# A long convolution by FFT beside local attention: the forward transforms in two passes, in place

## The chip, the core and the metric

The kernel runs on one core of a Trainium2 chip. The metric is the device time of one execution in microseconds (us); the table below gives the median of three executions. The profile is one further execution, whose span leaves out about 2 us that the device time has.

Five engines with their own instruction queues work in parallel and wait for each other through semaphores: TensorE (PE; its weight loads are shown apart as PEld), VectorE (DVE), ScalarE (ACT), GpSimd (POOL) and SyncE (SP, which here only issues transfers). TensorE writes its results to PSUM; ScalarE and VectorE copy them ("evict" them) to SBUF.

## The reference

Two branches share the input x and are mixed by a gate per position. S = 2048 positions, D = 640 channels, bfloat16.

```python
x = A_q
g = _sigmoid((x * gate_w).sum(-1, keepdims=True))
# branch a: short convolution of k (4 taps) times v, then a convolution with ssm_k as long as the sequence
kv = k_shift * v
kv_f = rfft(pad(kv, 2 * S));  kf_f = rfft(pad(ssm_k, 2 * S))        # along positions, per channel
y = irfft(kv_f * kf_f)[:S]
a = q * (y + kv * ssm_D)
# branch b: 32 heads of 20, each position attends to 8 positions at distance 0, 2, ..., 14
q, k, v = split(x @ wqkv);  b = softmax(q . k[idx] * scale) . v[idx] @ wo
out = g * a + (1 - g) * b
```

## The kernel before

The transform of 4096 points is done as two stages of small matmuls. Channels are held as 5 groups of 16 in the free dimension, 4 quarters and 2 halves, so that one tile of 4096 elements per partition is one group. Stage 1 ("s1") multiplies by `F1b`, stage 2 ("s2") by a matrix `G[:, j]` of its own for each of 32 frequencies j, with a real and an imaginary row (`rr`). The same code transforms h (the long filter) and u (the product k_shift * v).

```python
def s1_unit(key, src, g, oc, Am, free):          # 8 matmuls of 128 columns, one eviction of 1024
    ...
    copy(e.eng, Am[:, :, :, 4 * oc:4 * oc + 4]..., ps[:]...)

def s2_unit(dst, jb, Am, deps, free):            # one group, 8 frequencies: 32 matmuls of 64 columns
    for jj in range(8):
        j = 8 * jb + jj
        for rr in range(2):
            for c in range(2):
                rows = slice(64 * c, 64 * c + 64)
                o = ps[:, c, :].rearrange("p (q j l) -> p q j l", q=4, j=8)[:, :, jj, :]
                nc.tensor.matmul(o, lhsT=G[rows, j, rr, :], rhs=Am[rows, 2 * j + rr, :, :],
                                 start=(rr == 0), stop=(rr == 1), tile_position=(64 * c, 0), ...)
    copy(e.eng, dst[:, :, :, 8 * jb:8 * jb + 8, :]..., ps[:]...)   # one eviction of 1024

def transform(key, s2dst, s2free):               # s1 of group g+1 between s2 of group g
    for oc in range(4):
        yield from s1(0, oc)
    for g in range(NG):
        for jb in range(4):
            if g + 1 < NG:
                yield from s1(g + 1, jb)
            pdone, edone = yield from s2_unit(dst, jb, Am, evs, s2free(g, jb))
```

Stage 1 writes into one of two buffers `Am`, stage 2 from there into `Hs[g]` for h or, for u, into one buffer `Up` for all groups, which must have been multiplied before the next group may be written. The complex product needs h also with its partition halves swapped (`Hw`, by SyncE's transfers, line 844). VectorE multiplies per group and per quarter of the frequencies (lines 866 and 869):

```python
        for g in range(NG):
            for jb in range(4):
                nc.vector.tensor_tensor(v(Hs), v(Up), v(Hs), ALU.mult)
                nc.vector.tensor_tensor(v(Hw), v(Up), v(Hw), ALU.mult)
```

The first inverse stage ("i1", line 883) multiplies both products by `M`, 16 matmuls and one eviction for a quarter of a group; the second ("i2", line 960) uses `T`. The output projection of the attention ("op", line 999) runs per block of 128 positions, 16 blocks. Then y is multiplied by the gated x in `qg` and the attention is added, per two blocks, and stored:

```python
    def store(t):
        if t in (1, 5):
            return
        t0 = t - 3 if t < 8 else t - 1
        for gg in range(4):
            eng = nc.gpsimd if t < 4 and gg % 2 else nc.scalar if t == 15 and gg % 2 else nc.sync
            eng.dma_start(...)
```

The order on each engine is made while the program is built. Each part of the kernel is a generator that asks for an engine ("P", or "AD" for whichever of ScalarE and VectorE a small table of costs says is done first). `Plan` takes, of all that could go next, the one that can start first, with a handicap of 120 ns per unit of priority:

```python
                p = pri if r.pri is None else r.pri
                key = (st + 120.0 * p, p, k)
    ...
    plan.add(conv(), 6)
    plan.add(qkproj(), 3)
    plan.add(h_stream(), 5)
    plan.add(u_stream(), 5)
    plan.add(mults(), 1)
    plan.add(inverse1(), 4)
    ...
```

So the costs in `Plan` decide only the order; the chip then runs each queue in that order, waiting where data is not there. PSUM is used as four slots of two banks.

Of the kernel before, what the change touches and what calls it, by code (L numbers as in the profile page):

```python
# [48 lines left out]
def fft_consts():  # L49
# [3 lines left out]
    F1b = np.zeros((4, 32, 2, 64))  # L53
    for q in range(4):
        F1b[q, :, q % 2, :] = F1
# [89 lines left out]

MODE = dict(score_gen=1, h_stream=2, u_stream=2, inverse2=4)


class Plan:
# [33 lines left out]
    def fetch(self, st, cost, ins, keep=False):  # L183

        pages, t = list(self.page), st
        for c in range(len(pages), (self.count + ins) // 256 + 1):
            at = t + cost * (256 * c - self.count) / ins
            late = max(0.0, pages[-1] + 3500.0 - at)
            pages.append(at + late)
            t += late  # L190
        if keep:
            self.page, self.count = pages, self.count + ins
        return t + cost
# [10 lines left out]
    def run(self):  # L204
        while self.streams:
# [19 lines left out]
            self.at[e] = end  # L225
            if r.move:
                at = max(self.pipe, st + 1300.0)
                self.pipe = at + r.move
                g.done = Ev(self.pipe + 700.0, "X")
                self.lane[e].append(g.done.t)  # L230
# [13 lines left out]
def kernel(  # L244
# [280 lines left out]
    def vproj():  # L525
        for half in range(2):
            c0 = 320 * half
            for b0 in range(0, NB, 2):
                nb = min(2, NB - b0)
                g = yield Req("P", 5 * nb * 136.0, xdeps(min(3, (b0 + nb - 1) // 4)) + [ev(f"Wv{half}")], take=1, pri=2 if half == 0 else 4, ins=5 * nb)  # L530
# [7 lines left out]
                r = yield Req("AD", n=320 * nb, deps=[g.done], give=g.banks, pri=-2, lean=0.0)  # L538
# [36 lines left out]
    def qkproj():  # L575
        free = [None] * 5
        for ft in range(NDT):
            for w in range(2):
# [4 lines left out]
                for t0, banks in ((0, ((0, 4), (4, 4))), (8, ((8, 3), (11, 3))), (14, ((14, 3),))):  # L583
# [16 lines left out]
                    r = yield Req("AD", n=n * nb_, deps=deps, give=held, pri=-4, lean=0.0)  # L600
# [115 lines left out]
    def s1_unit(key, src, g, oc, Am, free):  # L716
        if key == "h":
            src = src + [ev("hd0" if IL * g + 4 * oc < 40 else "hd1")]
        r = yield Req("P", 380.0, src + [ev("consts")], take=1, ins=8)
# [11 lines left out]
        if g == NG - 1 and oc == 3:  # L731
            mark(f"{key}s1", r)
        e = yield Req("AD", n=1024, deps=[r.done, free], give=r.banks)
        copy(e.eng, Am[:, :, :, 4 * oc:4 * oc + 4].rearrange("p j (a q) l -> p a q j l", a=2),
             ps[:].rearrange("p a (l q j) -> p a q j l", l=4, q=2))
        return e.done

    def s2_unit(dst, jb, Am, deps, free):
        r = yield Req("P", 500.0, deps + [ev(f"G{jb}")], take=1, ins=32)
        ps = psum(r, "s2")  # L740
        for jj in range(8):
            j = 8 * jb + jj
            for rr in range(2):
                for c in range(2):
                    rows = slice(64 * c, 64 * c + 64)
                    o = ps[:, c, :].rearrange("p (q j l) -> p q j l", q=4, j=8)[:, :, jj, :]
                    nc.tensor.matmul(o, lhsT=G[rows, j, rr, :], rhs=Am[rows, 2 * j + rr, :, :],  # L747
                                     start=(rr == 0), stop=(rr == 1), tile_position=(64 * c, 0), skip_group_check=True)
        e = yield Req("AD", n=1024, deps=[r.done, free], give=r.banks)
        copy(e.eng, dst[:, :, :, 8 * jb:8 * jb + 8, :].rearrange("p c q j l -> p (c q) (j l)"),  # L750
             ps[:].rearrange("p c (q m) -> p (c q) m", q=4))
        return r.done, e.done

    def open_l2():
        if "p2" not in st:
            Lx.close()
            st["p2"] = ctx.enter_context(tc.tile_pool(name="p2", bufs=1, side="left", reuse_waits="tile"))
            st["Hs"] = []
            for g in range(NG - 1):
                Hsb = st["p2"].tile([128, 2, 4, 32, IL], BF, name="Hs", tag=f"Hs{g}")  # L760
                st["Hs"].append(Hsb)
            st["Hs"].append(sH[:, 0:4096].rearrange("p (c q j l) -> p c q j l", c=2, q=4, j=32))

    amfree = [Ev(0.0), Ev(0.0)]
    amk = [0]

    def h_stream():
        yield Req("G", 1000.0, [ev("qk"), ev("vproj1"), ev("conv0"), ev("gatePE")])
        open_l2()
        yield from transform("h", lambda g: st["Hs"][g], lambda g, jb: ev("frag") if g == NG - 1 else Ev(0.0))  # L770
# [9 lines left out]
    def transform(key, s2dst, s2free):  # L780

        ams = {}

        def s1(g, oc):
            if oc == 0:
                b = amk[0] % 2
                amk[0] += 1
                Am = st["p2"].tile([128, 64, 4, IL], BF, name="Am", tag=f"Am{b}")
                mine = Ev()
                ams[g] = (Am, amfree[b], mine, [])  # L790
                amfree[b] = mine
            Am, free, mine, evs = ams[g]
            d = yield from s1_unit(key, [], g, oc, Am, free)
            evs.append(d)

        for oc in range(4):
            yield from s1(0, oc)
        for g in range(NG):
            Am, _, mine, evs = ams[g]
            dst = s2dst(g)  # L800
            outs = []
            for jb in range(4):
                if g + 1 < NG:
                    yield from s1(g + 1, jb)
                pdone, edone = yield from s2_unit(dst, jb, Am, evs, s2free(g, jb))
                outs.append(edone)
            mine.t, mine.eng = pdone.t, "P"
            for k, o in enumerate(outs):
                x = ev(f"{key}{g}out{k}")
                x.t, x.eng = o.t, o.eng  # L810

    def outs(key, g):
        return [ev(f"{key}{g}out{k}") for k in range(4)]

    upfree = [Ev(0.0)] * NG

    def up_dst(g):
        Up = xpos(7)
        st[("Up", g)] = Up
        return Up  # L820

    def open_p3():
# [4 lines left out]
        st["X"] = X  # L827
        x = ev("p3"); x.t = 0.0

    def xpos(k):  # L830
        return st["X"][:, k, :].rearrange("p (c q j l) -> p c q j l", c=2, q=4, j=32)

    def u_stream():
        yield Req("G", 1.0, [ev("pv"), ev("hs1"), ev("kv0"), ev("kv1"), ev("p3")])
        yield from transform("u", up_dst, lambda g, jb: ev(f"m{g - 1}{jb}") if g else Ev(0.0))
# [6 lines left out]
    def swap(Hw, Hs, p):  # L842
        for d, h in zip(pieces(Hw.rearrange("p c q j l -> p (c q j l)")[p:p + 64]), pieces(Hs[:].rearrange("p c q j l -> p (c q j l)")[64 - p:128 - p])):
            nc.sync.dma_start(d, h)

    def swaps():
        for g in range(NG):
            r = yield Req("S", 1000.0, outs("h", g) + [ev("p3")], move=us(524288, 1024) * 1.9)
            Hs, Hw = st["Hs"][g], xpos(2 + g)
            st[("Hw", g)] = Hw  # L850
            swap(Hw, Hs, 0)
            r = yield Req("S", 1000.0, move=us(524288, 1024) * 1.9)
            swap(Hw, Hs, 64)
            mark(f"hw{g}", r)

    def mults():
        for g in range(NG):
            for jb in range(4):
                js = slice(8 * jb, 8 * jb + 8)
                r = yield Req("D", 660.0, [ev(f"u{g}out{jb}"), ev(f"h{g}out{jb}")])  # L860
                Hs, Up = st["Hs"][g], st[("Up", g)]

                def v(x):
                    return x[:, :, :, js, :].rearrange("p c q j l -> p (c q) (j l)")

                nc.vector.tensor_tensor(v(Hs), v(Up), v(Hs), ALU.mult)
                r = yield Req("D", 660.0, [ev(f"hw{g}")])
                Hw = st[("Hw", g)]
                nc.vector.tensor_tensor(v(Hw), v(Up), v(Hw), ALU.mult)  # L869
                mark(f"m{g}{jb}", r)  # L870
            mark(f"mult{g}", r)

    def inverse1():
        for g in range(NG):
            for c in range(2):
                for oc in range(2):
                    r = yield Req("P", 16 * 62.0, [ev(f"mult{g}")], take=1, ins=16)
                    Hs, Hw, X = st["Hs"][g], st[("Hw", g)], st["X"]
                    ps = psum(r, "i1")
                    for il in range(8):  # L880
                        o = ps[:, il // 4, 128 * (il % 4):128 * (il % 4) + 128]
                        for k, src in ((0, Hs), (1, Hw)):
                            nc.tensor.matmul(o, lhsT=src[:, c, :, :, 8 * oc + il].rearrange("p q j -> p (q j)"), rhs=M[:, k, :],  # L883
                                             start=(k == 0), stop=(k == 1), skip_group_check=True)
                    e = yield Req("AD", n=1024, deps=[r.done] + ([ev("bl5")] if g == 1 else []), give=r.banks)
# [3 lines left out]
            mark(f"cm{g}", e)  # L889
            if g == 0:  # L890
                T = st["p2"].tile([128, 64, 2, 32], BF, name="T", tag="Hs0")
                st["T"] = T
# [22 lines left out]
    def load_q():  # L915
# [3 lines left out]
        for a in range(2):  # L919
            for g in range(4):  # L920
                r = yield Req("S", 900.0, move=us(327680, 1280) * 1.5)
# [3 lines left out]
            mark(f"qg{a}", r)  # L925

    def load_t():
        r = yield Req("S", 500.0, [ev("i10")], move=us(1048576, 8192))
        for d, h in zip(pieces(st["T"][:].rearrange("p a r b -> p (a r b)")), pieces(cf["T"].ap())):
# [49 lines left out]
    def store(t):  # L979
        if t in (1, 5):  # L980
            return
        t0 = t - 3 if t < 8 else t - 1
        for gg in range(4):
            eng = nc.gpsimd if t < 4 and gg % 2 else nc.scalar if t == 15 and gg % 2 else nc.sync
# [3 lines left out]
    def outproj():  # L988
        yield Req("G", 1.0, [ev("oT"), ev("wo"), ev("gate")])
        oT, wo, bl = st["oT"], st["wo"], st["bl"]  # L990
        stage = None
        for t in range(16):
            u = t // 2
            g = yield Req("P", 1400.0, [ev(f"bl{2 * u - 5}")] if u >= 6 else [ev("i11")] if u >= 3 else [], take=1, ins=10, pri=8 if t < 8 else 0)
# [6 lines left out]
            if t == 6:  # L1001
                room = st["p2"].tile([128, 4096], BF, name="room", tag="Hs1")
# [94 lines left out]
```

## Time and profile before

| | |
|---|---|
| time | 250.64 us median of 3 (250.38 to 251.04) |
| profiled span | 248.4 us |
| TensorE busy | 211.4 us (85%), 4294 matmuls |
| VectorE busy | 178.4 us (72%) |
| ScalarE busy | 182.5 us (73%) |
| granted TensorE clock, mean | 0.896 |

Busy shares are averages over stages that differ. They are read by stage: which engine is full there, and what ended the waits of the one that is not. In a line of a group, the mean duration of one instruction holds its whole passage, so back-to-back matmuls overlap, and busy time, not the mean times the count, is what they took.

### The profile page before, as it was taken

Reading aid. Unit: us, or ns where it says so; the run is one execution under the profiler, and the core shown is the slowest. Engines: PE = TensorE matmul, PEld = TensorE weight load, DVE = VectorE, ACT = ScalarE, POOL = GpSimd, SP = SyncE. Lnnn points to the kernel's source line nnn. Section 1 sums busy time; section 2 is a strip of 40 time slices with the busy share of each in tenths; the row PEclk is TensorE's granted clock in tenths of the full one; section 3 lists DMA queues with packets and bytes.
Section 4 is the critical chain, followed back from the end, with each engine's and each line's share of the span. In section 5 each row is a group of like instructions: output and inputs, shape, how many; then the busy total and the mean of one; then the engine's idle time right before and its main releaser. Section 6 shows DMA issues by size and latency. Waiting matters only on the chain.

```text
span 248.4 us, 9692 instructions
## 1 busy us (share of the span) xinstructions
PE 211.4 (85%) x4294; PEld 160.9 (65%) x4294; DVE 178.4 (72%) x225; ACT 182.5 (73%) x218; POOL 67.7 (27%) x137
## 2 busy tenths in 40 slices
PE   7999989999999998888889569899979999995400
PEld 3765635655455666566769468889969999994300
DVE  0666879999999644578687667979597639946850
ACT  3437587767787799989998656689797978986810
POOL 7803703664251246340000000033030333033100
PEclk9999999999999999955556979999999999999555
DMA  6997499966697373898994856791140119951464
GB/s 185 354 338 272 114 312 349 280 145 180 109 184 156 96 185 83 196 233 152 284 326 86 197 109 149 159 217 58 57 172 3 55 40 227 205 121 55 137 175 116
DMA packets 51753, 42.67 MB, mean 172 GB/s; under 512 B 27280, under 2 KB 46864, under 8 KB 51712
## 3 DMA queue, kind: packets, MB, share of 16 engines
q1 hardware_dynamic: 46928, 32.87, 52.1%
q0 software_dynamic: 4688, 9.03, 14.1%
q8 instruction: 33, 0.54, 1.0%
q10 hardware_dynamic: 96, 0.16, 0.3%
q14 instruction: 8, 0.07, 0.1%
HBM read 23.51 MB, written 5.25 MB: 116 GB/s over the span
## 4 chain that ended last, share of the span: by engine, by line
PE 49%; DVE 18%; ACT 10%; issue 8%; DMA 7%; SPq 2%; POOL 1%; DVEq 0%; ACTq 0%
PE pj L596 11%; PE op L999 7%; PE i L883 7%; PE psv L534 6%; ACT ET L670 6%; PE s L747 5%; PE O L696 4%; DVE pb L474 4%; DVE pa L489 3%; PE s L729 3%; PE sc L662 3%; DMA qg<-in_A_q_dram 2%; DMA Wv<-in_B_wqkv_dram 2%; DVE Hb L273 2%; SPq L923 2%
## 5 line engine op out<-in xcount | busy, mean ns | idle before, releaser
L670 ACT ACTIVATE ET<-sc 128x726 bf16<-128x726 f32 (+1 forms) x80 | 64.5, 864 | 5.1 <-PE sc L662 4.7
L596 PE MATMUL pj<-xT,Wqk 128*128 128x363 bf16 (+3 forms) x250 | 48.4, 343 | 1.8 <-DVE oS L710 1.2
L596 PEld LDWEIGHTS <-Wqk 128*128 128x128 bf16 x250 | 23.0, 97 | 20.5 <-DVE oS L710 1.9
L747 PE MATMUL s<-Am,Gs 64*128 64x64 bf16 x1280 | 29.7, 201 | 6.4 <-issue 4.1
L747 PEld LDWEIGHTS <-Gs 64*128 64x128 bf16 x1280 | 26.5, 102 | 10.2 <-issue 9.0
L273 DVE CAST Am<-s 128x1024 bf16<-128x1024 f32 x20 | 23.9, 1219 | 6.3 <-PE s L729 6.3
L534 PE MATMUL psv<-Wv,xT 128*128 128x320 bf16 x170 | 25.2, 299 | 1.1 <-DMA Wv<-in_B_wqkv_dram 0.5
L999 PE MATMUL op<-wo,Hb 128*128 128x320 bf16 x160 | 25.1, 304 | 0.0
L883 PE MATMUL i<-M,X 128*128 128x128 bf16 x160 | 21.3, 227 | 0.5 <-DVE X L869 0.5
L271 ACT CAST Am<-s 128x1024 bf16<-128x1024 f32 x20 | 20.0, 1030 | 2.4 <-PE s L729 2.2
L271 ACT CAST X<-i 128x1024 bf16<-128x1024 f32 x19 | 19.1, 1012 | 3.4 <-PE i L883 2.3
L1019 POOL DMA_DIRECT2D bl<-X x12 | 6.3, 532 | 56.0 <-ACT X L1010 56.0
L999 PEld LDWEIGHTS <-Hb 128*128 128x128 bf16 x160 | 20.8, 146 | 0.7
L883 PEld LDWEIGHTS <-X 128*128 128x128 bf16 x160 | 20.4, 149 | 0.9 <-DVE X L869 0.9
L534 PEld LDWEIGHTS <-xT 128*128 128x128 bf16 x170 | 16.0, 98 | 7.6 <-issue 1.0
L662 PE MATMUL sc<-qb,kb 31*128 31x121 bf16 x544 | 18.6, 245 | 2.3 <-DVE oS L710 1.0
L1019 POOL DMA_DIRECT2D bl<-room x20 | 10.4, 526 | 33.9 <-ACT room L1010 33.9
L696 PEld LDWEIGHTS <-ET 128*128 128x128 bf16 x544 | 16.1, 100 | 5.1 <-issue 2.7
L696 PE MATMUL O<-VW,ET 128*128 128x21 bf16 x544 | 16.6, 176 | 2.5 <-ACT ET L670 1.5
L662 PEld LDWEIGHTS <-kb 31*128 31x128 bf16 x544 | 10.3, 103 | 12.1 <-issue 8.5
L489 DVE TENSOR_TENSOR pa<-pa,pb 128x2560 bf16<-128x2560 bf16 x12 | 17.9, 1489 | 0.3
L883 PE MATMUL i<-M,Hs 128*128 128x128 bf16 x128 | 17.1, 228 | 0.4 <-ACT X L271 0.4
(83 smaller groups left out, 380.1 us busy)
## 6 DMA issues: line engine op xcount, KB each, us to landing
X<-Hs SPq DMA_DIRECT2D x16, 256.0 KB, 5.6
Hb<-in_A_k_dram SPq DMA_DIRECT2D x4, 640.0 KB, 10.7
kv<-in_A_v_dram SPq DMA_DIRECT2D x4, 640.0 KB, 12.2
kv_scr<-Hb SPq DMA_DIRECT2D x8, 320.0 KB, 5.2
Hb<-in_A_ssm_k_dram SPq DMA_DIRECT2D x16, 160.0 KB, 5.3
kv<-kv_scr SPq DMA_DIRECT2D x8, 320.0 KB, 5.2
qg<-in_A_q_dram SPq DMA_DIRECT2D x16, 160.0 KB, 6.5
Gs<-cf_G SPq DMA_DIRECT2D x8, 256.0 KB, 7.3
```

The source lines that it names most:

```text
L271: nc.scalar.copy(dst, src)
L273: nc.vector.tensor_copy(dst, src)
L489: nc.vector.tensor_tensor(pa[:], pa[:], pb[:], ALU.add)
L534: nc.tensor.matmul(ps[:, bb, 0:320], lhsT=xT[:, dt, BP * (b0 + bb):BP * (b0 + bb) + 128], rhs=Wv[:, dt, c0:c0 + 320], start=(dt == 0), sto ...
L596: nc.tensor.matmul(ps[:, i, 0:n], lhsT=Wqk[:, dt, w, 128 * ft:128 * ft + 128], rhs=rhs, start=(dt == 0), stop=(dt == NDT - 1))
L662: nc.tensor.matmul(scs[h4 // 2][:, h4 % 2, BP * bb:BP * bb + BP], lhsT=kb[r:r + DH + NF, 128 * b:128 * b + 128], rhs=qb[r:r + DH + NF, BP ...
L670: nc.scalar.activation(ETs[e][:, :, 0:nw], scs[hf][:, :, 0:nw], ACT.Exp, scale=SCALE)
L696: nc.tensor.matmul(O[:, o0:o0 + 21], lhsT=ET[:, hh, BP * bb:BP * bb + 128], rhs=VW[:, b, 4 * t + h4, :], start=True, stop=True, skip_group ...
L747: nc.tensor.matmul(o, lhsT=G[rows, j, rr, :], rhs=Am[rows, 2 * j + rr, :, :], start=(rr == 0), stop=(rr == 1), tile_position=(64 * c, 0), ...
L883: nc.tensor.matmul(o, lhsT=src[:, c, :, :, 8 * oc + il].rearrange("p q j -> p (q j)"), rhs=M[:, k, :], start=(k == 0), stop=(k == 1), skip ...
L999: nc.tensor.matmul(op[:, k, 0:320], lhsT=raw(a, HS * (t % 2) + t // 2, [a.ap[0], [8, 128]]), rhs=wo[:, ft, 320 * k:320 * k + 320], start=( ...
L1019: nc.gpsimd.dma_start(bl[32 * gg:32 * gg + 32, t - 1:t + 1, :].rearrange("p t c -> p (t c)"), raw(row, 0, [[4 * pitch, 32], [1, 1280]]))
```

## The change

It has these parts.

1. The two stages are done in two passes, of groups 0 to 2 and of groups 3 and 4. A unit of stage 2 takes 2 (or 4) frequencies of all three (or two) groups of the pass at once, so a matmul has 192 (or 128) columns instead of 64.
2. Stage 1 lays out its result so that a frequency's real and imaginary parts lie where the result of that frequency will be put. Stage 2's eviction writes each frequency over its input. The buffers `Am` and `Up` go; all of u has its own place, and so u need not wait for products.
3. H's product with u is one instruction for all groups of a pass. The product with the swapped h is written over u instead of over the swapped copy.
4. The priorities, and leanings of single evictions to one engine or the other, come from a search and stand in a table `PR`. `HEAD` is new in the model of the plan: an engine is taken to be free a little before its instruction ends.
5. Stores are of four blocks up to block 11, then of two, and ScalarE issues half of those of blocks 12 to 15.
6. `T` is loaded into part of the swapped copy's place after the last product, and the staging place of the output projection is a tile of its own.

```diff
-    def s2_unit(dst, jb, Am, deps, free):
-        r = yield Req("P", 500.0, deps + [ev(f"G{jb}")], take=1, ins=32)
+    PASS = ((0, 3, 2), (3, 2, 4))
+
+    def s2_unit(key, ps_, k, A, deps):
+        g0, n, m = PASS[ps_]
+        r = yield Req("P", m * n * (66.0 if n > 2 else 70.0) + 60.0, deps + [ev(f"G{m * k // 8}")], take=1, ins=4 * m)
         ps = psum(r, "s2")
-        for jj in range(8):
-            j = 8 * jb + jj
+        for jj in range(m):
+            j = m * k + jj
             for rr in range(2):
                 for c in range(2):
                     rows = slice(64 * c, 64 * c + 64)
-                    nc.tensor.matmul(o, lhsT=G[rows, j, rr, :], rhs=Am[rows, 2 * j + rr, :, :],
+                    a = A[rows, g0, 0:1]
+                    nc.tensor.matmul(ps[:, c, 0:64 * n * m]..., lhsT=G[rows, j, rr, :],
+                                     rhs=raw(a, 2048 * rr + 16 * j, [a.ap[0], [4096, n], [512, 4], [1, 16]]),
                                      start=(rr == 0), stop=(rr == 1), tile_position=(64 * c, 0), ...)
-        copy(e.eng, dst[:, :, :, 8 * jb:8 * jb + 8, :]..., ps[:]...)
+        copy(e.eng, A[:, g0:g0 + n, :]...[:, :, :, :, 16 * m * k:16 * m * k + 16 * m], ps[:, :, 0:64 * n * m]...)
 ...
+    def transform(key, A):
+        for g in range(3):
+            yield from s1(g)
+        first = list(evs)
+        for k in range(16):
+            yield from s2_unit(key, 0, k, A, first)
+            if k in (0, 8):
+                yield from s1(3 + k // 8)
+        for k in range(8):
+            yield from s2_unit(key, 1, k, A, evs)
 ...
+                nc.vector.tensor_tensor(blocks(st["HA"]), blocks(st["UA"]), blocks(st["HA"]), ALU.mult)
+                for g in range(g0, g0 + n):
+                    nc.vector.tensor_tensor(U_, U_, block(turned(g)), ALU.mult)
 ...
     def store(t):
-        if t in (1, 5):
+        if t in (1, 5, 9):
             return
-        t0 = t - 3 if t < 8 else t - 1
+        t0 = t - 1 if t > 12 else t - 3
         for gg in range(4):
-            eng = nc.gpsimd if t < 4 and gg % 2 else nc.scalar if t == 15 and gg % 2 else nc.sync
+            eng = nc.gpsimd if t < 4 and gg % 2 else nc.scalar if t > 12 and gg % 2 else nc.sync
 ...
+PR = {..., 'conv': 17.2, 'qkproj': 3.1, 'h_stream': 1.9, 'u_stream': 7.3, 'mults': -6.7, 'inverse1': 11.0, 'opearly': 14.6, 'oplate': 22.1, 'vlean': 5.0, 'qlean': -169.0, 'slean': 204.0, 'ilean': 93.0, ...}
+HEAD = dict(A=130.0, D=60.0)
 ...
-    plan.add(conv(), 6)
+    plan.add(conv(), PR["conv"])
```

## The prediction

> **What bounds the kernel now.** I read four views in this order: the busy totals of the page, the windows cut at the kernel's own stage ends, the groups by line and form, and the timeline of the stages that turn out to be loose.
>
> The windows come first. The cuts are the end of the last V projection (101.5), the end of the last exponential (131.3), the last eviction of the h transform (160), the last of the first inverse stage (222) and the last add (239.4). Columns: window, its length, then busy us (count) of PE, PEld, DVE, ACT, POOL, then granted clock, DMA share, GB/s.
>
> ```profile
> 0.00:31.00 31.00, 29.14 (x222) 18.72 (x222) 17.61 (x17) 15.58 (x18) 16.88 (x41) 1.00 0.82 253
> 31.00:101.50 70.50, 66.56 (x897) 39.13 (x898) 58.16 (x65) 56.28 (x75) 28.47 (x54) 1.00 0.75 188
> 101.50:131.30 29.80, 25.06 (x664) 19.70 (x661) 21.40 (x31) 28.10 (x38) 4.54 (x9) 0.55 0.94 236
> 131.30:160.00 28.70, 22.63 (x753) 21.18 (x752) 21.89 (x23) 19.23 (x20) 0.00 (x0) 0.87 0.70 150
> 160.00:222.00 62.00, 60.35 (x1266) 56.24 (x1271) 45.04 (x67) 52.17 (x58) 14.65 (x28) 1.00 0.49 116
> 222.00:239.40 17.40, 7.65 (x522) 5.94 (x516) 14.29 (x25) 11.16 (x14) 3.11 (x6) 0.76 0.41 117
> 239.40:248.40 9.00, 0.00 (x0) 0.00 (x0) 0.03 (x1) 0.00 (x0) 0.00 (x0) 0.50 0.46 111
> ```
>
> Up to 101.5 TensorE is the bound (95.7 of 101.5 us). From 101.5 to 131.3 ScalarE is, with the exponentials (28.1 of 29.8). From 131.3 to 160 nothing is: TensorE, VectorE and ScalarE each work 19 to 23 of 28.7 us. From 160 to 222 TensorE is nearly full. At the end VectorE multiplies and adds, and then 9 us pass in which no engine computes.
>
> The loose stage is h's second forward stage. The timeline of TensorE there:
>
> ```profile
> 137.27 0.51 PE L747 MATMUL s<-Am,Gs 64*128 64x64 bf16 x23 [0.39 <-ACT Am L271]
> 139.75 0.32 PE L747 MATMUL s<-Am,Gs 64*128 64x64 bf16 x9 [1.97 <-issue]
> 142.51 0.62 PE L747 MATMUL s<-Am,Gs 64*128 64x64 bf16 x31 [0.27 <-DVE Hs L273]
> 145.12 0.20 PE L747 MATMUL s<-Am,Gs 64*128 64x64 bf16 x1 [1.99 <-issue]
> ```
>
> Twice TensorE stops for 2 us in the middle of a run of small matmuls with no data missing: the wait is "issue". The groups by line and form give the unit costs (busy us, mean ns | idle before):
>
> ```profile
> L747 PE MATMUL s<-Am,Gs 64*128 64x64 bf16 x1280 | 29.7, 201 | 6.4 <-issue 4.1 <-DVE Hs L273 0.7 <-ACT Am L271 0.4
> L273 DVE CAST Am<-s 128x1024 bf16<-128x1024 f32 x20 | 23.9, 1219 | 6.3 <-PE s L729 6.3
> L271 ACT CAST Am<-s 128x1024 bf16<-128x1024 f32 x20 | 20.0, 1030 | 2.4 <-PE s L729 2.2
> L271 ACT CAST Gs<-pj 128x768 bf16<-128x768 f32 x2 | 1.6, 800 | 1.8 <-PE pj L596 1.8
> L273 DVE CAST Gs<-pj 128x768 bf16<-128x768 f32 x1 | 1.0, 951 | 0.0
> L866 DVE TENSOR_TENSOR Hs<-X,Hs 128x1024 bf16<-128x1024 bf16 x16 | 10.9, 684 | 0.0
> ```
>
> And the end, where SyncE issues all but four of the stores and is not done until 245.3:
>
> ```profile
> 229.30 16.02 SPq L985 DMA_DIRECT2D out_dram<-qg  x20
> 239.46 0.85 ACTq L985 DMA_DIRECT2D out_dram<-qg  x2
> ```
>
> **What the Trainium skill says.** "Runtime: NRT & Kernel Launch", section "Instruction fetch mechanics": TensorE's instructions come in blocks of 256, fetched while the block before runs, mostly hidden. Here it is not always hidden: between the two stops above the timeline counts 9 + 8 + 32 + 8 + 32 + 8 + 31 = 128 matmuls, each with its weight load, so exactly 256 instructions. I take the stops for waits on the next block; the page supports it, the trace itself says only "issue".
> "VectorE: DVE Perf Modes", section "The perf-mode tier table": `tensor_tensor` with a PSUM operand runs at the plain rate, bf16 in SBUF at twice that. The trace agrees for PSUM as a source (1219 ns for 1024 fp32 elements) and for SBUF (684 ns for 1024).
>
> **The change, part by part.**
>
> *Matmuls of the second stage.* A unit was 32 matmuls of 64 columns, 20 units per transform. The chain of waits shows one undisturbed unit at 0.57 us, so 11.4 us per transform. Now a pass over three groups has 16 units of 8 matmuls of 192 columns, and a pass over two has 8 units of 16 matmuls of 128: 256 matmuls instead of 640. Two matmuls run side by side on the halves of the rows, so a pass-one unit is 4 pairs. The V projection runs 10 x 320 columns in 1.36 us, 0.425 ns a column; 192 columns are 82 ns, 85 with a margin, 0.34 us a unit. In pass two 8 pairs at 60 ns are 0.48 us. Sum 16 x 0.34 + 8 x 0.48 = 9.3 us. That is 2.1 us less per transform, 4.2 in all, and 1536 fewer instructions in TensorE's stream (768 matmuls and their loads).
>
> *Evictions.* First stage: 20 of 1024 per transform, as before. Second: 20 of 1024 become 16 of 768 and 8 of 1024, the same elements with four more fixed costs. ScalarE and VectorE together clear 1024 elements each 0.56 us (1/1.02 + 1/1.22 per us) and 768 each 0.435 us: 40 x 0.56 = 22.4 us before, 28 x 0.56 + 16 x 0.435 = 22.6 after. No gain: the work is the same, only its placing can help.
>
> *Multiplications.* Twenty H multiplications of 1024 become four of 3072 and four of 2048; the other twenty stay. From 684 ns for 1024 and 1489 for 2560, a slope of 0.52 ns; 1.75 and 1.22 us give 11.9 instead of 13.7 us.
>
> *Order.* Built, the new program has the order of each engine. Up to the last exponential, TensorE no longer runs the three second-stage units (32 matmuls, 1.03 us each at the halved clock) that stood between scores, and does two more first-stage units; conv ranks lower on VectorE, so the attention divisions free PSUM sooner. The stage until 101.5 is full of TensorE work that stays; from then on 33 exponentials are left instead of 35. I take the last exponential at 129 instead of 131.3.
>
> From there ScalarE has, in order: for h, 5 x 1.03 + 9 x 0.80 + 4 x 1.02 = 16.4 us; for u, 13 x 1.03 + three transposes of attention output 3 x 1.68 + 11 x 0.80 + 8 x 1.02 + 4 output projections x 0.80 = 38.6; for the first inverse stage 20 x 1.01 + 2 x 0.80 = 21.8. Sum 76.8 us. VectorE beside it has 18 us for h and about 43 for u: its last product comes some 61 us after the exponentials, and is needed only by the fourth group of the inverse stage, after 16.4 + 38.6 + 12 x 1.01 = 67 us of ScalarE. TensorE needs about 12 us for h and 26 for u: also less. ScalarE is the chain. I add 5 us for its gaps: one refill at the start of each transform's second stage (all 12 first-stage evictions must be in), banks, and a slow clock in h's stage. 129 + 76.8 + 5 = 210.8, where before the same point is 221.7: 90.4 us become 81.8.
>
> *Tail.* Now ten output projections are left for TensorE after the first inverse stage, where two were. Ten at 1.45 us and 512 small matmuls at 10.8 ns are 20 us, starting 1.2 us before the last eviction. VectorE follows: per group of three blocks four products straight from PSUM, 480 elements at the PSUM rate, about 0.65 us each by the rows above, and 1.3 adds of 0.82 us: 3.7 us against TensorE's 4.0, so it keeps up. After the last matmul there are two copies, a product and an add, 3.4 us; then two store issues on each of two queues 0.8, landing 1.9 (the median of the stores now) and the 1.2 us from the last landing to the end: 3.9. So 20 - 1.2 + 3.4 + 3.9 = 26.1 us, where before it is 248.4 - 221.7 = 26.7. Inside that, the 9 us after the last add become about 4, because 14 stores instead of 20 stand on SyncE, but the ten projections eat it.
>
> *Sum.* 210.8 + 26.1 = 236.9 us of span; the timed median is 2.2 above the profiled span (250.64 against 248.4): 239.1. I round up to 240.0, as the order is fixed and every slip adds.
>
> **Rivals.**
> (1) *The order is a plan and the chip slips.* Two passes mean that no second-stage unit starts before all 12 first-stage evictions of the pass; if h's data (loaded behind the four later convolution stores) come late, the queue of TensorE stands. For it: conv 0 moves behind two more attention parts on VectorE, and h's second half landed at 120.6 before, needed now at about 126. It would cost 3 to 6 us: 243 to 246.
> (2) *TensorE's clock.* It was 0.55 in the exponentials' stage and 0.87 after. At half clock a pass-one unit is 0.68 us against 0.435 of evicting, and h's stage becomes TensorE's: 4 to 6 us more, 244 to 246.
> (3) *The gain is larger.* If the early stage also tightens (TensorE waited there for VectorE's divisions behind 1.5 us conv pieces), the last exponential comes at 126 and the end at 236.
> (4) *Nothing is gained*, because the evictions bound everything: 22.6 us against 22.4. Against it: ScalarE idles 9.5 of 28.7 us in h's stage and 10 of 62 after.
>
> **Range and chances.** Terms: the exponentials' end +-2.5, ScalarE's gaps +6/-3, tail +-3. Together 235 to 246.5. Two per cent faster is 245.6; it takes rival 1 or 2 nearly in full to miss it. Faster 0.87, within 2% 0.11, slower 0.02.
>
> **What would show it.** Right: the "issue" stops in h's second stage gone; last exponential near 129; h's last eviction near 147 instead of 160; last eviction of the first inverse stage near 211 with ScalarE over 90% busy from 129 on; TensorE busy about 6 us less in sum; store issues ended within 2 us of the last add. Wrong: VectorE or TensorE full and ScalarE with gaps of microseconds between 129 and 211, the first h unit waiting for data, or a clock near half in h's stage.

## The result, and the profile after

The changed kernel takes 240.69 us, the median of four executions (238.44 to 242.58); the kernel before took 250.84 beside it. The ratio is 0.954 with an interval of 0.943 to 0.965. Executions of one kernel fall into a faster and a slower state; ratios here use the faster alone, while the profiled execution, with a span of 240.7 us, is of the slower (the other three span 236.7 to 238.9 us).

The windows, cut again at the stage ends (the last V projection, the last exponential, h's last eviction on ScalarE, the last of the first inverse stage, the last add). Columns as in the prediction: window, length, busy us (count) of PE, PEld, DVE, ACT, POOL, then granted clock, DMA share, GB/s.

```profile
100.60:129.80 29.20, 21.77 (x540) 16.31 (x537) 21.16 (x31) 25.56 (x34) 4.55 (x9) 0.57 0.97 208
129.80:146.40 16.60, 15.12 (x361) 12.97 (x358) 16.11 (x19) 15.22 (x18) 0.00 (x0) 0.93 0.46 151
146.40:209.80 63.40, 57.41 (x884) 53.03 (x882) 45.66 (x61) 55.61 (x61) 6.28 (x12) 0.95 0.78 153
209.80:234.60 24.80, 18.27 (x605) 16.32 (x603) 17.69 (x28) 10.51 (x14) 11.43 (x22) 0.93 0.55 161
234.60:240.70 6.10, 0.00 (x0) 0.00 (x0) 0.02 (x1) 0.00 (x0) 0.00 (x0) 0.50 0.20 54
```

The largest difference is in one place. h's stage, 28.7 us before, takes 16.6, with all three compute engines over 90% busy. The exponentials end 1.5 us earlier. u's stage and the first inverse stage together take 63.4 us (62.0 before), and from there to the end it is 30.9 us (26.4 before between the same two cuts), so the tail gives 4.5 us back: -1.5 - 12.1 + 1.4 + 4.5 = -7.7, the difference of the spans. The cuts do not enclose the same work, though: 85 transposes of attention output (5.1 us of TensorE) ran inside h's stage before and run in u's now, and ten output projections of 1.45 us follow the first inverse stage instead of two. So the 12.1 us are not all won in h's stage; what is, an experiment below shows with the order kept.

TensorE's timeline in h's second stage, where two "issue" stops of 2 us stood before:

```profile
133.38 3.69 PE L760 MATMUL s<-Hs,Gs 64*128 64x192 bf16 x64 [0.29 <-ACT Hs L277]
...
139.42 6.61 PE L760 MATMUL s<-Hs,Gs 64*128 64x192 bf16 x176 [0.40 <-DVE Hs L279]
```

Long rows now run through, and the short waits between them name the engine that evicts. The groups by line and form:

```profile
L760 PE MATMUL s<-Hs,Gs 64*128 64x192 bf16 x128 | 7.3, 250 | 0.9 <-DVE Hs L279 0.4 <-ACT Hs L277 0.3
L760 PE MATMUL s<-Hs,Gs 64*128 64x128 bf16 x128 | 4.2, 216 | 0.1
L858 DVE TENSOR_TENSOR Hs<-X,Hs 128x2048 bf16<-128x2048 bf16 x4 | 4.9, 1220 | 6.5 <-DMA X<-Hs 6.5
```

256 matmuls of h take 11.5 us; u's two forms show 7.1 and 4.4. The third line holds something the kernel before did not have: a product of VectorE that waited 6.5 us for a transfer. The timeline of SyncE's queue ahead of it:

```profile
171.28 7.68 SPq L911 DMA_DIRECT2D qg<-in_A_q_dram  x12
179.53 1.40 SPq L844 DMA_DIRECT2D X<-Hs  x2
```

VectorE's timeline, the product itself:

```profile
191.24 1.23 DVE L858 TENSOR_TENSOR Hs<-X,Hs 128x2048 bf16<-128x2048 bf16 x1 [6.45 <-DMA X<-Hs]
```

ScalarE's timeline soon after:

```profile
200.08 1.01 ACT L277 CAST X<-i 128x1024 bf16<-128x1024 f32 x1 [4.13 <-PE i L875]
```

The product overwrites h's spectrum, so it must wait until the swap of that part of h (the last half of group five) has read it. That swap stands in SyncE's queue behind twelve loads of `qg`, is issued at 179.53 and releases the product at 191.2. TensorE then runs out of products, and ScalarE stands 4.1 us for TensorE. Not all of the stage's delay is this wait: from 198.2 to 203.8 the matmuls of the first inverse stage start every 0.107 us instead of 0.063. In the run with the old stores below, whose order up to here is the same, the wait is 6.3 us and ScalarE's 3.3, the granted clock in this stage is 1.00, and the stage from u's last eviction takes 24.5 us where it takes 27.0 here. A column "idle before" of 6.5 us on an engine that isn't the bound would cost nothing; here the third line shows that it reached the bound.

The end of the chain that ended last:

```profile
226.87 0.80 ACT room L995
227.67 0.28 issue
227.95 1.55 POOL bl L1004 x3
229.51 4.17 DMA bl<-room
...
233.79 0.82 DVE qg L1012
```

After the last output projection its eviction, the issue of its four gathering transfers (`bl`), their 4.2 us and one add follow each other; the stores and 6.1 us more come after that.

### The profile page after: what moved, and what is told of

It reads as the page before. It is cut to its first block, busy times and chain, and to the rows that moved or that the text cites. A ratio compares the mean times of both kernels' runs of the same rounds, so it can differ in the third digit from the quotient of the medians.

```text
span 240.7 us, 8121 instructions
## 1 busy us (share of the span) xinstructions
PE 209.9 (87%) x3526; PEld 157.5 (65%) x3526; DVE 172.4 (72%) x214; ACT 183.6 (76%) x225; POOL 67.7 (28%) x137
## 4 chain that ended last, share of the span: by engine, by line
PE 43%; DMA 17%; ACT 14%; SPq 9%; DVE 7%; issue 4%; POOL 3%; DVEq 0%; ACTq 0%
PE pj L602 13%; DMA qg<-in_A_q_dram 9%; SPq L359 8%; PE psv L540 8%; PE op L988 6%; ACT X L277 6%; DVE Hs L279 5%; PE i L875 4%; ACT ET L676 4%; PE sc L668 3%; PE s L760 2%; DMA Wv<-in_B_wqkv_dram 2%; ACT Hb L277 2%; DMA bl<-room 2%; PE O L702 2%
## 5 line engine op out<-in xcount | busy, mean ns | idle before, releaser
L1004 POOL DMA_DIRECT2D bl<-room x32 | 16.7, 528 | 84.0 <-ACT room L995 84.0
L279 DVE CAST Hs<-s 128x1024 bf16<-128x1024 f32 (+1 forms) x26 | 28.6, 1143 | 2.5 <-PE s L738 2.4
L277 ACT CAST X<-s 128x1024 bf16<-128x1024 f32 (+1 forms) x32 | 28.0, 1000 | 0.2 <-PE s L738 0.2
L875 PE MATMUL i<-M,Hs 128*128 128x128 bf16 x160 | 22.9, 241 | 2.5 <-DVE Hs L858 2.3
L875 PE MATMUL i<-M,X 128*128 128x128 bf16 x160 | 22.8, 241 | 0.5 <-DVE X L862 0.5
L875 PEld LDWEIGHTS <-Hs 128*128 128x128 bf16 x160 | 21.4, 152 | 2.7 <-DVE Hs L858 2.6
L760 PEld LDWEIGHTS <-Gs 64*128 64x128 bf16 x512 | 18.4, 95 | 5.7 <-issue 5.0
L995 ACT ACTIVATE room<-op,omg 128x640 bf16<-128x640 f32 x16 | 13.2, 826 | 10.3 <-PE op L988 10.3
L638 POOL DMA_DIRECT2D qb<-Gs x21 | 11.4, 549 | 32.9 <-ACT Gs L277 20.7
L965 DVE TENSOR_TENSOR qg<-i,qg 128x480 bf16<-128x480 f32 x16 | 9.4, 649 | 12.5 <-PE i L950 12.5
```

The lines of the kernel that those rows point to most:

```text
L277: nc.scalar.copy(dst, src)
L279: nc.vector.tensor_copy(dst, src)
L760: nc.tensor.matmul(ps[:, c, 0:64 * n * m].rearrange("p (a j l) -> p a j l", j=m, l=16)[:, :, jj, :], lhsT=G[rows, j, rr, :], rhs=raw(a, 20 ...
L875: nc.tensor.matmul(o, lhsT=piece(A[:, g:g + 1, :])[:, 0, c, :, :, 8 * oc + il].rearrange("p q j -> p (q j)"), rhs=M[:, k, :], start=(k == ...
L1004: nc.gpsimd.dma_start(bl[32 * gg:32 * gg + 32, t - 1:t + 1, :].rearrange("p t c -> p (t c)"), raw(row, 0, [[4 * pitch, 32], [1, 1280]]))
```

## Experiments

Each is the changed kernel with the edit shown, unless the text says otherwise. The kernel before took 250.9 to 251.2 us (median) beside them; ratios are to it.

### What the wide matmuls are worth

Both transforms cut back to matmuls of 64 columns, everything else kept:

```diff
-nc.tensor.matmul(ps[...n groups...], lhsT=G[rows, j, rr, :], rhs=<n groups of A>, ...)
+for g in range(n):
+    nc.tensor.matmul(ps[...group g...], lhsT=G[rows, j, rr, :], rhs=<group g0+g of A>, ...)
```

> The changed kernel, but each matmul of the second forward stage is split back into one per group: 64 columns, 1280 instead of 512, with a weight load each. Evictions, order and priorities stay. Theory (fewer instructions in TensorE's stream free h's stage): 2 us stops of the kind 'issue' come back in h's second stage, the time from the last exponential to h's last eviction grows from 16.6 to about 21 us, and the whole is 4 to 7 us slower, 245 to 247. Rival (the width of the matmuls is beside the point, evictions set the stage's length in both kernels): within 1.5 us of 240.7.

Measured: 251.29 us, 0.9999 (0.9962 to 1.0036): the whole gain is gone, 10.6 us where 4 to 7 were expected. TensorE's timeline in h's stage:

```profile
146.50 2.04 PE L761 MATMUL s<-Hs,Gs 64*128 64x64 bf16 x128 [1.69 <-issue]
151.87 1.06 PE L761 MATMUL s<-Hs,Gs 64*128 64x64 bf16 x33 [3.33 <-issue]
```

From one stop to the next there are exactly 128 matmuls, each with its weight load, so 256 instructions. Two such blocks took 2.0 us, one 2.4; after them TensorE stands 1.7, 3.3 and 1.1 us with no data missing. h's last eviction, on VectorE, ends at 154.2 instead of 147.6. The Trainium skill ("Runtime: NRT & Kernel Launch", section "Instruction fetch mechanics") describes blocks of 256 instructions for TensorE; the length of the rows agrees with it, while its "mostly hidden" does not hold for blocks that run in 2.0 us. The waits say only "issue", but the transfers in the trace name the cause. The page of the profile has a queue of the kind "instruction" (columns: packets, MB, share of the 16 engines); first the kernel before, then the changed one:

```profile
q8 instruction: 33, 0.54, 1.0%
q8 instruction: 27, 0.44, 0.8%
```

Its packets are of 16 KB. The 33 match TensorE's 2 x 4294 matmuls and weight loads in blocks of 256 (33.5 of them), the 27 its 2 x 3526 (27.5); this edit has 33 again. And they match in time: here the packets end at 141.4, 145.2 and 150.5, and TensorE goes on at 142.8, 146.5 and 151.9. In the 13 traces at a normal clock TensorE has 42 "issue" stops of 0.5 us or more, and each ends 1.1 to 1.8 us after such a packet has landed. So the stops are waits for the next block of instructions.

The order was searched for the wide matmuls, so another order might win back a part of the loss; that was not tried.

Only h's transform cut back, u's left wide (the same edit under `if key == "h"`):

> The changed kernel with only h's second stage cut back to matmuls of 64 columns (640 instead of 256); u's stays at 192 and 128. With both cut back it took 251.3, with none 240.7. Theory (TensorE's stops come in h's stage, where its small matmuls run with nothing between them, and what is lost there is not made up later): h's last eviction 6 to 8 us later, near 154, and 247 to 249 us in all; u's stage as fast as in the changed kernel. Rival (the swap of h's last group is bound to the transfers, so a later h is absorbed in the 6.5 us for which the product waits): under 245.

Measured: 249.13 us, 0.991 (0.987 to 0.994). The windows from the last exponential to h's last eviction, to u's, and to the end of the first inverse stage:

```profile
130.70:155.50 24.80, 16.52 (x746) 15.16 (x744) 16.90 (x20) 15.47 (x19) 0.00 (x0) 0.84 0.52 144
155.50:193.10 37.60, 34.32 (x572) 30.47 (x568) 34.49 (x36) 34.97 (x40) 4.22 (x8) 0.94 0.77 147
193.10:218.10 25.00, 23.21 (x321) 22.79 (x320) 11.12 (x25) 20.75 (x22) 2.18 (x4) 0.93 0.57 122
```

and those of the changed kernel from u's start, for comparison:

```profile
146.40:182.80 36.40, 33.19 (x566) 29.27 (x564) 34.09 (x37) 34.79 (x40) 4.20 (x8) 1.00 0.94 179
182.80:209.80 27.00, 24.22 (x322) 23.75 (x320) 11.57 (x25) 20.82 (x23) 2.08 (x4) 0.87 0.55 117
```

h's stage is 24.8 us with the same busy times of VectorE and ScalarE (16.9 and 15.5) as in the 16.6 us of the changed kernel: 8.2 us in which they wait for TensorE, whose busy time has grown by only 1.4 us, while its "issue" stops there add up to 7.8 us. So the stops cost it, not the matmuls' own time. The following stages give back 0.8 us of it; 8.4 us of the time are lost, four fifths of the change's gain. The other 2 us of the first experiment belong to u's transform, where first-stage units and transposes stand between.

### What the searched order is worth

The old priorities, no leanings (which engine takes an eviction), no head start, the old fetch constant:

```diff
-PR = {... 'mults': -6.7, 'outproj': 6.2, 'opearly': 14.6, 'qlean': -169.0, 'slean': 204.0, ...}
+PR = {... 'mults': 1.0, 'outproj': 6.0, 'opearly': 8.0, 'qlean': 0.0, 'slean': 0.0, ...}
-HEAD = dict(A=130.0, D=60.0)
+HEAD = dict(A=0.0, D=0.0)
```

> The changed kernel with the old plan: priorities of before, no leanings, no early release of ScalarE and VectorE in the model. The two passes, the wide matmuls, the merged products and the stores of four blocks stay. Theory (two passes make the work denser, and ScalarE is the chain from the last exponential on): most of the 10 us stays, 242 to 245 us, because the forward stages of h still run without stops of TensorE. Rival (the searched order is what gains, the passes only cost nothing): 247 us or more.

Measured: 254.52 us, 1.016 (1.008 to 1.025): slower than the kernel before, though h's second stage has no "issue" stops here either. The theory falls. VectorE's timeline:

```profile
172.10 1.76 DVE L858 TENSOR_TENSOR Hs<-X,Hs 128x3072 bf16<-128x3072 bf16 x1 [5.21 <-ACT room L995]
```

At 172 the first product stands in VectorE's queue ahead of evictions that it could do, and waits for ScalarE, which evicts output projections; TensorE then waits 4.3 us for VectorE. h's stage takes 29 us, with TensorE 26.6 of them at work, because u's first-stage units and transposes stand between h's.

The plan cut in two. The old priorities with the new leanings, head start and constant:

> The changed kernel with the priorities of the kernel before, but with the new leanings (which engine takes an eviction), the new head start and the new fetch constant. With all of the old plan it took 254.5, with all of the new 240.7. Theory (the order is what matters: a product ahead of u's evictions in VectorE's queue, u's first stage and transposes of attention output between h's units, no output projections left for the end): the time stays near the old plan's, 250 to 255. Rival (the balance of evictions between ScalarE and VectorE is what the search found): 241 to 246.

Measured: 259.83 us, 1.038 (1.033 to 1.044). And the new priorities without those:

> The changed kernel with the new priorities, but without the leanings, the head start and the new fetch constant: the other cut through the plan. All old 254.5, old priorities with new leanings 259.8, all new 240.7. Theory (the priorities carry the plan's gain): 241 to 245. Rival (only both together work, since the leanings were searched with them): over 248.

Measured: 253.39 us, 1.012 (1.004 to 1.019). Each half alone is slower than the old kernel. In the second, the window of h's stage:

```profile
129.30:152.90 23.60, 19.09 (x396) 16.14 (x394) 18.35 (x21) 17.60 (x21) 0.56 (x1) 0.79 0.62 187
```

and TensorE's timeline at its start:

```profile
131.68 1.21 PE L738 MATMUL s<-F1b,Hb 64*128 64x128 bf16 x16 [1.56 <-POOL Hb L802]
```

The filter's loads are issued until 128.6 instead of 123.9, so the first stage waits for its data, the second for the first, and the clock is 0.79 instead of 0.93: 7.0 of the 11.2 us between the spans are in this stage. I had held one half to be the carrier; the runs show that neither is. Which of leanings, head start and constant the priorities need was not separated.

### The wait for the swap

The `qg` loads issued behind the last swap:

```diff
-r = yield Req("S", 900.0, [ev("us1")], move=us(327680, 1280) * 1.4)
+r = yield Req("S", 900.0, [ev("us1"), ev("hw43")], move=us(327680, 1280) * 1.4)
```

> The changed kernel, but the loads of the gated x (16 transfers of 160 KB) are issued behind the last swap of h's fifth group instead of before it. Theory (VectorE's 6.5 us wait before the third product of pass two is the swap's transfers standing in the queue behind these loads, and it delays the fourth and fifth group of the first inverse stage): the wait falls under 2 us, the inverse stage ends 4 to 5 us earlier, 236 to 237 us. Rival 1 (the wait is hidden, ScalarE would have been late anyway): within 1 us of 240.7. Rival 2 (the loads now come late themselves, and the scaling of x holds the second inverse stage): 240 or more with a wait of VectorE for these loads.

Measured: 237.05 us, 0.949 (0.941 to 0.958). The wait of 6.5 us is gone, the last product ends at 188.4 instead of 198.8 and the first inverse stage at 201.1 instead of 209.8. The order of the edited kernel also leaves eleven instead of ten projections for the tail, which takes some of it back. Its interval overlaps that of the changed kernel; what carries the reading is that all ten executions with late loads (these and six below) lie between 236.2 and 238.9 us, the fourteen with early loads between 237.3 and 242.7. Measured against VectorE's products beside it, the swap was issued only about 1 us late in the changed kernel. The rest is its landing: up to 10.8 us from issue behind the loads' 1.9 MB, at most 5.7 us here.

### The tail and the stores

The stores as before the change, in the changed kernel (20 on SyncE, 2 on ScalarE at the end):

> The changed kernel with the store scheme of before (stores of two blocks from block 8 on, all but two by SyncE). Theory (the stores do matter, but the output projections in the tail now spread them out): 1 to 2 us slower, 242 to 243, with SyncE issuing for some us after the last add. Rival (in the tail of this order they are hidden): within 0.7 us of 240.7.

Measured: 240.69 us, 0.964 (0.954 to 0.974): the same as with the new stores. And the new stores alone in the kernel before:

> The kernel before with the new stores alone: SyncE's queue has 10 of four blocks and 4 of two, ScalarE's 4, in place of 20 and 2. Theory of the prediction (20 stores on one queue make 9 us after the last add, fewer make about 4): 3 to 5 us gained, 246 to 248. Rival (the changed kernel with the old stores took the same as with the new, so the number of stores sets nothing): within 1 us of 250.8; or slower, if the larger stores start later.

Measured: 248.56 us, 0.996 (0.992 to 0.9995). From the last add to the end 6.6 us instead of 9.0, but about 1 us of time by the ratio. So fewer stores on one queue help the old tail a little; in the new tail no gain is seen, though four executions with an interval of 1% to each side could hide 1 us.

Block 13's stores moved out of ScalarE's queue, where they stood ahead of the last two copies, which had waited 2.6 us for no named cause:

```diff
-eng = ... nc.scalar if t > 12 and gg % 2 else nc.sync
+eng = ... nc.scalar if t == 15 and gg % 2 else nc.sync
```

> The changed kernel in which ScalarE's queue issues only the last block's two stores; block 13's two go to SyncE's queue. Nothing else differs in any engine's order. Theory (the tail is 4.8 us longer than predicted, and 2.6 us of it is ScalarE standing in front of its last two copies because block 13's stores, which wait for an add on VectorE, are ahead of them in its queue): the 2.6 us stop goes, the last block's copy, product and add come earlier, and 1.5 to 2.5 us are gained: 238 to 239.5. Rival (the last bl transfer sets the end, so the copies may come earlier for nothing): under 0.7 us, 240 to 241.

Measured: 241.37 us, 0.951 (0.943 to 0.959): nothing. ScalarE's stop is gone, and VectorE's last add shows what had been behind it:

```profile
232.99 0.83 DVE L1012 TENSOR_TENSOR qg<-qg,bl 128x1280 bf16<-128x1280 bf16 x1 [1.83 <-DMA bl<-room]
```

The add waits 1.83 us for the last gather, where it waited 0.50, and 6.5 us follow it. The median is the rival's, and the trace agrees with it: the gather sets the end. With late `qg` loads as well:

> The changed kernel with both: the qg loads behind the last half swaps of h in SyncE's queue, and block 13's stores on SyncE. Theory (two separate waits, one in the inverse stage and one in the tail): 237.05 less another 2 us, 234.5 to 236. Rival (the tail is set by the transfers, or the stops overlap): no better than 236.8.

Measured: 237.02 us, 0.947 (0.943 to 0.951), so the late loads alone do it. Again the rival's number. All six executions lie between 236.4 and 237.5, under all four of the changed kernel. Its window from u's last eviction to the end of the first inverse stage, to be set beside 182.80:209.80 above:

```profile
182.30:202.30 20.00, 20.00 (x311) 20.00 (x310) 11.74 (x25) 19.97 (x21) 0.00 (x0) 1.00 0.94 198
```

TensorE and ScalarE are both busy throughout, in 20 us instead of 27 (24.5 at full clock), one projection's eviction of about 1 us having moved out of it: in this order the stage has no idle time left on either. From here on the edits stand on this version. Eight output projections instead of five before the end of this stage:

```diff
-'opearly': 14.6
+'opearly': 5.0
```

> The version with late qg loads and block 13's stores on SyncE, with the first eight output projections given a higher rank: eight instead of five run before the end of the first inverse stage, so eight instead of eleven are left after it. Theory (the tail is a row on TensorE of projections and inverse matmuls, 20.7 us there, followed by one gather, add and store): the row is 3 x 1.45 = 4.4 us shorter, ScalarE does three more evictions of 0.8 earlier, net 1.5 to 2.5 us gained, 234.5 to 235.5. Rival (the stage before is full on ScalarE and the tail is bound by the gathers): 236.5 or more.

Measured: 238.97 us, 0.951 (0.943 to 0.959): no gain seen, the rival's number. The profiled execution ran at about half the clock throughout and its trace is not used, so what became of the three projections is open. With all sixteen ahead of the tail (`'oplate': 0.0` as well):

> The same with all sixteen projections ranked ahead of the first inverse stage, so that the 512 small matmuls of the last stage (1024 instructions, four blocks of 256) follow each other with nothing between. Theory: they no longer run at 10.8 ns each, 5.5 us, but stop for the next block of instructions, 2 us or more in each of three or four blocks (in the run with the old plan the last stage had 5.0 us of such stops), and VectorE's 16 us of products and adds have nothing left to overlap: 236 to 240. Rival (the tail shrinks by the ten projections, 14 us of TensorE, and only some 9 us of it come back as evictions earlier): 232 to 235.

Measured: 241.65 us, 0.967 (0.960 to 0.973): the theory's direction, 1.7 us beyond its range. The first inverse stage ends at 215.5 instead of 202.3, and the last stage on TensorE now reads:

```profile
215.56 1.49 PE L950 MATMUL i<-X 32*32 32x160 bf16 x135 [1.10 <-ACT X L277]
219.24 1.62 PE L950 MATMUL i<-X 32*32 32x160 bf16 x128 [2.19 <-issue]
222.97 1.85 PE L950 MATMUL i<-X 32*32 32x160 bf16 x123 [2.11 <-issue]
```

Again about 128 matmuls and their loads are one row. From one row's start to the next it is 3.7 us, of which 1.5 to 1.6 are matmuls. A projection, ten matmuls of 0.14 us, costs few instructions for its time; in the changed kernel, with projections between the inverse matmuls, this line has no "issue" wait at all (4.3 us in the kernel before). The sum: the stages up to 215.5 are 13.2 us longer, the rest is 24.2 us instead of 33.5, so 9.3 us shorter, with 5.0 us of stops in it.

## Why the prediction was right

It gave 240.0 us for 240.69. By its steps, in the profiled execution:

- *Last exponential at 129*: 129.8.
- *h's last eviction near 147, the stops gone*: 146.4 on ScalarE, 147.6 on VectorE, and gone. The mechanism was right and is shown by taking the wide matmuls away from h alone (8.4 us). But the prediction put the matmuls at "4.2 in all" and did not price the stops, whose loss sat in the difference between 160 and 147. The fewer instructions were the gain, not the shorter TensorE time.
- *Second stage, 9.3 us per transform*: 11.5. The pair of 192-column matmuls takes 0.111 us, not 0.085 (7.1 us for 64 pairs at full clock). Little of it reached the sum: from 131.6 to 146.4 the timeline of ScalarE's evictions shows a single gap, of 0.23 us.
- *ScalarE's chain, 76.8 + 5 = 81.8 us*: 80.0 from 129.8 to 209.8. Two errors cancel. Its 79 instructions occupy 15.2 + 55.6 = 70.8 us, 6.0 fewer, since their durations overlap (they add up to 80.4); its gaps are 9.2: 1.4 in h's stage, 1.6 in u's (36.4 - 34.8) and 6.2 in the inverse stage (27.0 - 20.8). "One refill at the start of each transform's second stage, banks, and a slow clock" covers the first two; the third was the swap behind the `qg` loads, and the slower matmuls after it, which no rival named (2.4 us of it are absent from the run with the old stores, where the chain takes 77.6). The order of SyncE's queue had been there to read before the run. Two of its own signs went against it here: a gap of 4.1 us on ScalarE, which it had listed under wrong, and ScalarE at 89% instead of over 90%.
- *Tail 26.1*: 30.9. The row on TensorE was right (18.8 from the last eviction to the last matmul; measured 228.07 - 209.79 = 18.3). The products straight from PSUM took 0.65 us each, as estimated (0.66 for twice the elements from SBUF); the cast of 1219 ns that it had quoted beside the rate of `tensor_tensor` is another instruction. The term of 3.4 + 3.9 for what follows was 12.6. "Two copies, a product and an add" is not the path: eviction, gather and add of the last projection are, and the gather's 0.28 + 1.55 + 4.17 us were left out. The 9 us after the last add became 6.1, not about 4; the stores' landing has a median of 2.7 us in place of 1.9, in part because more of them are of 160 KB (those of 80 KB: 2.4 to 2.5 in place of 1.8), and what fills the rest is not shown.
- *TensorE about 6 us less busy*: 211.4 to 209.9. The second stage fell by 6.7 us (29.7 to 23.0), but the first inverse stage grew from 42.8 to 45.7 in a window with a clock of 0.87 (41.1 in the run with the old stores, with 207.9 in all); the rest is spread.

Rival 1 (late data for h) and rival 2 (half clock in h's stage) did not occur here; rival 1 did with the searched leanings taken out. Rival 3 (the last exponential at 126) and rival 4 (nothing gained) did not occur either. The number owes much to luck. The worked span of 236.9 us is 3.8 under the profiled 240.7 (+0.8, -1.8 and +4.8 by the steps above) and 2.0 under the 238.9 of the middle executions. The rounding up gave back 0.9, and the conversion from span to time 0.4: it was taken as 2.2, from a median and a profile of different executions, and is 1.8 within one.

## What to carry to other kernels

Count the instructions of a stage of small matmuls as well as its time: where 256 of them run in less than the 3.5 to 5.4 us that lay between the starts of two such blocks here, fewer and wider matmuls, or long ones set between, can be worth more than the matmul time saved. An in-place scheme adds a reader that each overwriting waits for; put that reader's transfer ahead of loads that nobody needs yet (late loads: 237.0 us instead of 240.7). A new data layout and the order of the queues are one change: here the layout with the old order was slower than the old kernel.

## What the runs showed of the hardware

- TensorE's stops for instructions follow blocks of 256: 1.1 us after a block that ran in 2.4 us, 1.7 and 3.3 us after blocks of 2.0 us, 2.1 to 2.2 us after blocks of the last stage that ran in 1.5 to 1.6 us. With all matmuls of 64 columns a block's 16 KB packet starts 1.1 us after the first matmul of the block before it (3.0 us once), takes 0.9 to 1.3 us, and TensorE goes on 1.3 to 1.4 us later: 3.5 to 3.7 us from block to block, once 5.4. The kernel before has 5.4 us between its two stops, although the block itself took 3.4 us.
- ScalarE's evictions overlap in places: in u's stage the next one starts 0.69 us after one that lasts 0.86.

```profile
164.75 0.86 ACT L277 CAST X<-s 128x768 bf16<-128x768 f32 x1
165.44 0.86 ACT L995 ACTIVATE room<-op,omg 128x640 bf16<-128x640 f32 x1
```

- An 80 KB gather landed after a median of 2.6 us in the kernel before and 3.1 in the changed one, and the last took 4.2; why is not shown.
